# A recurrent attention layer on one core: the value pass in 32 rows, the memory-free tail tokens of four segments in one job, scores and softmax in two halves of the heads

## The chip, the cores and the metric

The kernel runs on one core of a Trainium2 chip. The metric is device time in microseconds for the whole program. "TensorE" is the matmul engine (PE in the profile, PEld its weight loads), VectorE is DVE, ScalarE is ACT, GpSimd is POOL, SP issues most of the DMAs.

## The reference, cut to what matters

Four layers, A B A B, on 2048 tokens of width 640. Layer A is not touched. Layer B is a recurrence over 64 segments of 32 tokens. Eight memory tokens stand before each segment, and the first eight output rows of a segment are the next segment's memory:

```
for s in range(64):
    h = concat([mem, x[32*s : 32*s+32]])          # 40 tokens, width 640
    q, k, v = h @ Wq, h @ Wk, h @ Wv              # 32 heads of 128 each
    p = softmax(mask(q k^T * scale))              # 40 x 40 per head
    o = (p v) @ Wo
    mem = o[:8];  outs.append(o[8:])
```

Only `mem` ties a step to the next. What depends on `x` alone can be computed ahead.

## The kernel before

Thirty-two stationary columns (tokens) use a quarter of TensorE's 128 columns, so four matmuls with different weights stand side by side (`tile_position`). Such a "thin group" of 20 matmuls covers half of one weight matrix:

```python
def thin_mm(cols_ap, Wt, b, name):                # 32 tokens, half b of the weights
    ps = ps_tile([128, 512], F32, name)
    for c in range(NCH):                          # 5 chunks of 128 of the width 640
        for j in range(4):
            n = 4 * b + j
            nc.tensor.matmul(ps[32*j:32*j+32, :], lhsT=cols_ap[:, c, :], rhs=Wt[:, c, 512*n:512*n+512],
                             start=(c == 0), stop=(c == NCH-1), tile_position=(0, 32*j), ...)
```

Queries and keys of a step are made for 32 columns: the 8 memory tokens, and the first 24 tokens of the *next* segment. The last 8 tokens of each segment (the "tail") come from a separate job, two segments at a time, half of it in each step as filler (`b_tps`). Values need all 40 tokens at once, so they go in 64 columns, two matmuls side by side, in four quarters:

```python
def v_quarter(b4):
    vps = ps_tile([128, 512], F32, "b_VPS")
    for c in range(NCH):
        for jj in range(2):
            n = 2 * b4 + jj
            nc.tensor.matmul(vps[64*jj:64*jj+64, :], lhsT=hT[s][:, c, 0:64], rhs=W.wv[:, c, 512*n:512*n+512],
                             start=(c == 0), stop=(c == NCH-1), tile_position=(0, 64*jj), ...)
```

The order of one step on TensorE, with the tile names that the profile shows:

```
Qa Qb Ka Kb | VPS 0 | TPQ | VPS 1 | TPK | SP (mask, scores) of both halves | VPS 2, 3
| tps | PTP (transposes of P) | tps | OTP (P times V) | OPS (output pass) | ttp | MT (memory to hT) | XPS (fold)
# every fourth step, serially after it:
| OPSd (output pass of the eight rows per segment that OPS leaves out, four segments at once) | wait for ScalarE | XPSd (fold)
# cut: softmax on VectorE, ScalarE and GpSimd, copies out of PSUM, DMAs
```

OPS handles 32 of a segment's 40 rows: the memory and 24 tokens. The other eight rows are collected over four segments; their OPSd is called the deferred pass below. MT writes the new memory into the next step's `hT`, and the next Qa waits for it. That is the recurrence.

Of the kernel before, what the change touches and what calls it, by code (L numbers as in the profile page):

```python
# [8 lines left out]
"""Dev version of the kernel (layer A / layer B building blocks)."""  # L9
# [19 lines left out]
D = 640  # L29
# [461 lines left out]
def b_group_of_head(h):  # L491
    pr = h // 2
    u, v = divmod(pr, 4)
    return 4 * u + (0, 2, 1, 3)[v]


def layer_B(nc, tc, C, W, x_src, xb_src, x_dst, mem0, nsteps=64, out_bf16=False, dbg=None):
    SCB = 1.0 / math.sqrt(128.0)
    nc_raw = nc
    nc = _OrdNC(tc, nc_raw, engines=ORDER_ENGINES)  # L500
    with ExitStack() as ctx:
        st = ctx.enter_context(tc.tile_pool(name="b_state", bufs=1))
        hp = ctx.enter_context(tc.tile_pool(name="b_hT", bufs=4))
        qkp = ctx.enter_context(tc.tile_pool(name="b_qk", bufs=4))
        wk = ctx.enter_context(tc.tile_pool(name="b_wk", bufs=1))
        wk2 = ctx.enter_context(tc.tile_pool(name="b_wk2", bufs=2))
        sm = ctx.enter_context(tc.tile_pool(name="b_sm", bufs=2))
# [8 lines left out]
        fold = st.tile([128, 2, 32], BF16, name="b_fold")  # L516
        nc.vector.tensor_tensor(out=fold[:, 0, :], in0=C.identb[:, 0:32], in1=C.identb[:, 64:96], op=ALU.add)
        nc.vector.tensor_tensor(out=fold[:, 1, :], in0=C.identb[:, 32:64], in1=C.identb[:, 96:128], op=ALU.add)
        OTdef = st.tile([128, 32, 32], BF16, name="b_OTdef")
        XO = st.tile([128, 320], F32, name="b_XO")  # L520
        nc.vector.memset(XO[:], 0.0)
        mask8 = st.tile([128, 8, 40], BF16, name="b_mask8")
        Pt = st.tile([128, 16, 64], BF16, name="b_P")
        nc.gpsimd.memset(Pt[:], 0.0)
# [4 lines left out]
        for hh in range(2):  # L529
            nc.gpsimd.affine_select(out=maskf[64 * hh:64 * hh + 32, 0:32], in_=negs[64 * hh:64 * hh + 32, :],  # L530
                                    pattern=[[1, 32]], compare_op=ALU.is_gt, fill=0.0, base=0, channel_multiplier=-1)
        nc.vector.tensor_copy(mask8[:], maskf[:].unsqueeze(1).to_broadcast([128, 8, 40]))

        xnT_g = {}
        ln_state = {}

        ln_dma = {}

        def ln_group_dma(g):
            xt = wk.tile([128, D], BF16, name="b_xt", tag="Qsb")  # L540
            nc.sync.dma_start(xt[:], xb_src[128 * g:128 * g + 128, :])
            ln_dma[g] = xt

        def ln_group_a(g):
            if g not in ln_dma:
                ln_group_dma(g)
            xt = ln_dma.pop(g)
            xn = wk.tile([128, D], BF16, name="b_xn", tag="PTsb")
            layernorm_tile(nc, sm, C, xt[:], xn[:], "b_ln")
            ln_state[g] = xn  # L550

        def ln_group_b(g):
            xn = ln_state.pop(g)
            tps = ps_tile([128, NCH, 128], BF16, "b_lntps")
            for c in range(NCH):
                nc.tensor.transpose(tps[:, c, :], xn[:, 128 * c:128 * c + 128], C.identb[:])
            xg = wk2.tile([128, NCH, 128], BF16, name="b_xnTg")
            nc.scalar.copy(xg[:], tps[:])
            xnT_g[g] = xg
# [5 lines left out]
        hT = {}  # L565
        QT = {}
        KT = {}

        def alloc_seg(s):
            hT[s] = hp.tile([128, NCH, 64], BF16, name="b_hT", tag="hT")  # L570
            QT[s] = qkp.tile([128, 32 * 40 + 24], BF16, name="b_QT", tag="QT")
            KT[s] = qkp.tile([128, 32 * 40 + 24], BF16, name="b_KT", tag="KT")
            nc.gpsimd.memset(QT[s][:, 1280:1304], 0.0)
            nc.gpsimd.memset(KT[s][:, 1280:1304], 0.0)
            nc.gpsimd.tensor_copy(hT[s][:, :, 0:32], xcols(s, 0, 32))
            if s >= 1 and (s - 1) in hT:
                nc.gpsimd.tensor_copy(hT[s - 1][:, :, 40:64], xcols(s, 0, 24))
            if s == nsteps - 1:
                nc.gpsimd.memset(hT[s][:, :, 40:64], 0.0)

        def thin_mm(cols_ap, Wt, b, name):
            ps = ps_tile([128, 512], F32, name)
            for c in range(NCH):
                for j in range(4):
                    n = 4 * b + j
                    nc.tensor.matmul(ps[32 * j:32 * j + 32, :], lhsT=cols_ap[:, c, :], rhs=Wt[:, c, 512 * n:512 * n + 512],
                                     start=(c == 0), stop=(c == NCH - 1), tile_position=(0, 32 * j), skip_group_check=True)
            return ps

        def evac(eng, dst, src, scale=None):  # L590
            if eng == "act":
                if scale is None:
                    nc.scalar.copy(dst, src)
                else:
                    nc.scalar.activation(out=dst, in_=src, func=ACT.Copy, scale=scale)
            elif eng == "dve":
                if scale is None:
                    nc.vector.tensor_copy(dst, src)
                else:
                    nc.vector.tensor_scalar(out=dst, in0=src, scalar1=scale, scalar2=None, op0=ALU.mult)  # L600
            else:
                nc.gpsimd.tensor_copy(dst, src)

        def transp4(sb_half, tp, b):
            for i in range(4):
                nc.tensor.transpose(tp[:, 4 * b + i, :], sb_half[:, 128 * i:128 * i + 128], C.identb[:])

        def scatter(eng, tp, b, dst_t, t0, t1, c0):
            src = tp[:, 4 * b:4 * b + 4, :].rearrange("p i (j t) -> p i j t", j=4)[:, :, :, t0:t1]
            dst = dst_t[:, 0:1280].rearrange("p (h c) -> p h c", c=40)[:, 16 * b:16 * b + 16, c0:c0 + (t1 - t0)] \  # L610
                .rearrange("p (j i) c -> p i j c", j=4)
            evac(eng, dst, src)

        def bulk_unit_pe(job, u):
            nm, b = (("Q", 0), ("Q", 1), ("K", 0), ("K", 1))[u]
            Wt = W.wq if nm == "Q" else W.wk
            job["ps"][u] = thin_mm(job["cols"], Wt, b, "b_tps")

        def bulk_unit_evac(job, u, eng):
            nm, b = (("Q", 0), ("Q", 1), ("K", 0), ("K", 1))[u]  # L620
            sb = wk.tile([128, 512], BF16, name="b_tsb", tag="tsb")
            evac(eng, sb[:], job["ps"][u][:], SCB if nm == "Q" else None)
            job["sb"][u] = sb

        def bulk_unit_tr(job, u):
            nm, b = (("Q", 0), ("Q", 1), ("K", 0), ("K", 1))[u]
            tp = ps_tile([128, 8, 128], BF16, "b_ttp")
            transp4(job["sb"][u][:], tp, 0)
            job["tp"][u] = tp

        def bulk_unit_scatter(job, u, eng):
            nm, b = (("Q", 0), ("Q", 1), ("K", 0), ("K", 1))[u]
            for (t0, t1, seg, c0) in job["dests"]:
                dst_t = (QT if nm == "Q" else KT)[seg]
                src = job["tp"][u][:, 0:4, :].rearrange("p i (j t) -> p i j t", j=4)[:, :, :, t0:t1]
                dst = dst_t[:, 0:1280].rearrange("p (h c) -> p h c", c=40)[:, 16 * b:16 * b + 16, c0:c0 + (t1 - t0)] \
                    .rearrange("p (j i) c -> p i j c", j=4)
                evac(eng, dst, src)

        def new_job(cols, dests):  # L640
            return {"cols": cols, "dests": dests, "ps": {}, "sb": {}, "tp": {}}

        def run_job_now(job):
            for u in range(4):
                bulk_unit_pe(job, u)
                bulk_unit_evac(job, u, "act" if u % 2 == 0 else "dve")
                bulk_unit_tr(job, u)
                bulk_unit_scatter(job, u, "dve" if u % 2 == 0 else "act")

        ln_group_a(0); ln_group_b(0)  # L650
        alloc_seg(0)
        with nc.allow_non_contiguous_dma(reason="mem0 transpose load (tiny)"):
            for c in range(NCH):
                nc.sync.dma_start(hT[0][:, c, 32:40], mem0[:, 128 * c:128 * c + 128].rearrange("t p -> p t"))
        if nsteps > 1:
            alloc_seg(1)
        run_job_now(new_job(hT[0][:, :, 0:32], [(0, 32, 0, 0)]))

        def make_tails_job(t):
            segs = [u for u in (t, t + 1) if u < nsteps]  # L660
            hx = wk.tile([128, NCH, 32], BF16, name="b_hx")
            nc.gpsimd.memset(hx[:], 0.0)
            dl = []
            for ii, u in enumerate(segs):
                nc.gpsimd.tensor_copy(hx[:, :, 8 * ii:8 * ii + 8], xcols(u, 24, 32))
                dl.append((8 * ii, 8 * ii + 8, u, 24))
            return new_job(hx[:], dl)

        if nsteps > 1:
            if nsteps > 2:  # L670
# [307 lines left out]
```

## Time and profile before

Median 3664.33 us (4 runs, 3661.93 to 3667.35).

| What | us | Where read |
|---|---|---|
| TensorE busy | 3322.3 of 3665.9 (91%) | page, part 1 |
| steps of layer B, in fours (the first listed is the second of a group) | 19.13, 19.13, 22.19, 19.26; mean 19.93 | timeline, start of Qa to start of Qa |
| 128 such steps | 2551, 70% of the span | product |
| value pass b_VPS | 626.3 | page, part 5 |

First the engines' busy time (page, part 1) and two costly groups (part 5: line, engine, operation, output from inputs, shapes, count, then busy us and mean ns of one, then idle time before them). All of layer B has line L103, a helper, so one goes by tile names.

```profile
PE 3322.3 (91%) x54915; PEld 2072.4 (57%) x54996; DVE 2032.6 (55%) x5299; ACT 1852.8 (51%) x4369; POOL 580.5 (16%) x1457
...
L103 PE MATMUL b_VPS<-b_wv,b_hT 128*64 128x512 bf16 x5120 | 626.3, 382 | 0.0
...
L103 PE MATMUL b_OPS<-b_wo,b_OTsb 128*32 128x320 bf16 x8192 | 304.5, 302 | 33.7 <-DVE b_OTsb L103 33.7
```

Now one step of the kernel before in the timeline, TensorE only, with some rows left out: start, duration, what, and in brackets how long the engine idled before it and for whom. It is one of the steps with the deferred pass.

```profile
1008.49 1.26 PE L103 MATMUL b_Qa<-b_wq,b_hT 128*32 128x512 bf16 x20
1009.57 1.25 PE L103 MATMUL b_Qb<-b_wq,b_hT 128*32 128x512 bf16 x20
...
1013.30 1.27 PE L103 MATMUL b_VPS<-b_wv,b_hT 128*64 128x512 bf16 x10
1014.50 0.62 PE L103 MATMUL b_TPQ<-c_identb,b_Qsb 128*128 128x128 bf16 x8
...
1018.12 2.35 PE L103 MATMUL b_VPS<-b_wv,b_hT 128*64 128x512 bf16 x20
1020.40 1.26 PE L103 MATMUL b_tps<-b_wq,b_hx 128*32 128x512 bf16 x20
1021.60 0.63 PE L103 MATMUL b_PTP<-c_identb,b_P 128*128 128x128 bf16 x8
1022.16 1.26 PE L103 MATMUL b_tps<-b_wq,b_hx 128*32 128x512 bf16 x20
1023.36 0.73 PE L103 MATMUL b_OTP<-b_PTsb,b_Vsb 40*128 40x40 bf16 x32
1024.31 2.36 PE L103 MATMUL b_OPS<-b_wo,b_OTsb 128*32 128x320 bf16 x64 [0.22 <-DVE b_OTsb L103]
...
1027.61 2.47 PE L103 MATMUL b_OPSd<-b_wo,b_OTdef 128*32 128x320 bf16 x64
1030.67 0.31 PE L103 MATMUL b_XPSd<-b_msbd,b_fold 128*32 128x320 bf16 x2 [0.59 <-ACT b_msbd L103]
1030.68 0.61 PE L103 MATMUL b_Qa<-b_wq,b_hT 128*32 128x512 bf16 x6
```

Read the *starts*, not the durations: matmuls are pipelined, and the last one's end is modelled. Qa starts at 1008.49 and Qb at 1009.57, so a thin group occupies TensorE for 1.08 us. A value quarter, half as many matmuls, takes as long: 64 columns allow two side by side, not four. When another tile shape follows, the same quarter needs 1.20 us (1013.30 to 1014.50). Between 1008.49 and 1030.68 hardly anything idles: TensorE carries the step. The deferred pass adds 3.06 us to every fourth step.

### The profile page before, as it was taken

What the parts mean: (1) busy time and instruction counts of PE and PEld (TensorE: products, weight loads), DVE (VectorE), ACT (ScalarE), POOL (GpSimd) and SP (SyncE); (2) the same over time, 40 slices, a digit from 0 to 9 for tenths busy, and PEclk for the clock granted to TensorE, in tenths of its full rate; (3) what the DMA queues carried; (4) which work ended last, traced back from release to release, by engine and by line L of the source; (5) the groups of instructions that cost most, each with busy time, mean ns of one, the idle gap of its engine ahead of it and who ended that gap; (6) DMA issues with size and microseconds to landing.
All of it is one profiled execution on the core that took longest, in us unless ns stands there. A gap on an engine that the chain in (4) does not pass through costs nothing.

```text
span 3665.9 us, 126295 instructions
## 1 busy us (share of the span) xinstructions
PE 3322.3 (91%) x54915; PEld 2072.4 (57%) x54996; DVE 2032.6 (55%) x5299; ACT 1852.8 (51%) x4369; POOL 580.5 (16%) x1457
## 2 busy tenths in 40 slices
PE   6988959999999999999869889599999999999998
PEld 4756635555555555555546666355555555555555
DVE  8888834444444444444479888344444444444444
ACT  5978824444444444444359788334444444444443
POOL 4233210110111111010122332101101110110100
PEclk9999979999999999999989999799999999999999
DMA  2010060000000000000020111600000000000000
GB/s 63 12 38 30 29 251 28 12 12 13 13 13 13 13 13 12 14 12 10 20 66 12 46 38 30 250 28 10 10 11 11 10 10 12 11 10 12 10 9 8
DMA packets 85997, 112.26 MB, mean 31 GB/s; under 512 B 27328, under 2 KB 75456, under 8 KB 81600
## 3 DMA queue, kind: packets, MB, share of 16 engines
q1 hardware_dynamic: 85440, 104.18, 9.0%
q8 instruction: 430, 7.05, 0.8%
q14 instruction: 127, 1.04, 0.1%
HBM read 72.13 MB, written 23.59 MB: 26 GB/s over the span
## 4 chain that ended last, share of the span: by engine, by line
PE 73%; ACT 12%; DVE 8%; issue 3%; DMA 2%; POOL 2%; SPq 0%; DVEq 0%; ACTq 0%; POOLq 0%
PE b_VPS L103 16%; PE b_tps L103 9%; PE b_OPS L103 8%; ACT a_Pj L338 5%; PE b_Qa L103 4%; PE b_Qb L103 4%; PE b_Ka L103 4%; PE b_Kb L103 4%; PE a_S L333 2%; ACT b_KT L103 2%; PE b_ttp L103 2%; PE b_PTP L103 2%; PE b_TPK L103 2%; PE b_TPQ L103 2%; PE b_OPSd L103 2%
## 5 line engine op out<-in xcount | busy, mean ns | idle before, releaser
L103 PEld LDWEIGHTS <-b_hT 128*32 128x32 bf16 (+1 forms) x15520 | 609.3, 102 | 499.2 <-issue 102.1
L103 PE MATMUL b_VPS<-b_wv,b_hT 128*64 128x512 bf16 x5120 | 626.3, 382 | 0.0
L338 ACT ACTIVATE a_Pj<-a_S,a_negm 128x128 bf16<-128x128 f32 (+3 forms) x1024 | 504.1, 541 | 49.1 <-DVE a_negm L337 42.9
L337 DVE TENSOR_REDUCE a_negm<-a_S 128x1 f32<-128x128 f32 (+3 forms) x1024 | 466.9, 481 | 76.8 <-PE a_S L335 48.8
L103 ACT CAST b_Vsb<-b_VPS 128x512 bf16<-128x512 f32 x512 | 289.3, 594 | 179.6 <-PE b_VPS L103 179.6
L103 POOL TENSOR_TENSOR b_P<-b_P,b_rs 128x320 bf16<-128x320 bf16 x128 | 92.4, 722 | 1799.7 <-DVE b_rs L103 1785.1
L103 PE MATMUL b_OPS<-b_wo,b_OTsb 128*32 128x320 bf16 x8192 | 304.5, 302 | 33.7 <-DVE b_OTsb L103 33.7
L103 PEld LDWEIGHTS <-b_OTsb 128*32 128x32 bf16 x8192 | 208.4, 97 | 99.9 <-DVE b_OTsb L103 46.8
L348 PE MATMUL a_tpA<-c_identb,a_Pj 128*128 128x128 bf16 x2048 | 232.1, 220 | 7.9 <-ACT a_Pj L338 2.8
L335 PE MATMUL a_S<-c_negu,c_identb 128*128 128x128 bf16 x1024 | 221.3, 219 | 0.0
L103 PEld LDWEIGHTS <-b_hx 128*32 128x32 bf16 x5120 | 114.0, 97 | 151.1 <-issue 56.0
L103 DVE CAST b_Ksb<-b_Kb 128x512 bf16<-128x512 f32 x128 | 88.5, 692 | 187.7 <-PE b_Kb L103 187.7
L103 DVE CAST b_OTsb<-b_OTP 128x320 bf16<-128x320 f32 x256 | 114.1, 486 | 141.4 <-PE b_OTP L103 141.0
L103 DVE COPY b_QT<-b_TPQ 128x128 bf16<-128x128 bf16 (+1 forms) x254 | 62.1, 286 | 231.3 <-ACT b_QT L103 231.3
L103 DVE TENSOR_SCALAR b_Qsb<-b_Qb 128x512 bf16<-128x512 f32 x128 | 88.5, 692 | 163.9 <-PE b_Qb L103 163.9
L103 ACT CAST b_Ksb<-b_Ka 128x512 bf16<-128x512 f32 x128 | 74.9, 585 | 206.7 <-PE b_Ka L103 206.7
L348 PEld LDWEIGHTS <-a_Pj 128*128 128x128 bf16 x2048 | 146.7, 97 | 50.3 <-issue 10.1
L103 PE MATMUL b_Qa<-b_wq,b_hT 128*32 128x512 bf16 x2560 | 167.3, 384 | 3.1
L335 PEld LDWEIGHTS <-c_identb 128*128 128x128 bf16 x1024 | 99.4, 97 | 124.7 <-issue 94.9
L103 PE MATMUL b_Qb<-b_wq,b_hT 128*32 128x512 bf16 x2560 | 165.7, 382 | 0.0
L103 PE MATMUL b_tps<-b_wq,b_hx 128*32 128x512 bf16 x2560 | 164.9, 387 | 0.0
L103 PE MATMUL b_Ka<-b_wk,b_hT 128*32 128x512 bf16 x2560 | 164.0, 379 | 0.0
(1623 smaller groups left out, 6161.5 us busy)
## 6 DMA issues: line engine op xcount, KB each, us to landing
xres<-a_xnew SPq DMA_DIRECT2D x32, 320.0 KB
b_wq<-in_B_Wq_dram SPq DMA_DIRECT2D x2, 5120.0 KB
b_wk<-in_B_Wk_dram SPq DMA_DIRECT2D x2, 5120.0 KB
b_wv<-in_B_Wv_dram SPq DMA_DIRECT2D x2, 5120.0 KB
b_wo<-in_B_Wo_dram SPq DMA_DIRECT2D x2, 5120.0 KB
b_XO<-xres SPq DMA_DIRECT2D x256, 30.0 KB
xres_bf<-a_xnb SPq DMA_DIRECT2D x32, 160.0 KB
b_xt<-xres_bf SPq DMA_DIRECT2D x32, 160.0 KB
```

The lines of the kernel that those rows point to most:

```text
L103: r = f(*a, **k)
L333: nc.tensor.matmul(Sx[:, 0:N], lhsT=stt["qTm"][:, j, 128 * qc:128 * qc + 128], rhs=kT[:, 0:N], start=True, stop=False)
L335: nc.tensor.matmul(Sx[:, N - 128:N], lhsT=C.identb[:], rhs=C.negu[:], start=False, stop=True)
L337: nc.vector.tensor_reduce(out=negm[:], in_=Sx[:, 0:N], axis=AX.X, op=ALU.max, negate=True)
L338: nc.scalar.activation(out=Pj[:, OFFS[qc]:OFFS[qc] + N], in_=Sx[:, 0:N], func=ACT.Exp, bias=negm[:, 0:1], scale=1.0)
L348: nc.tensor.transpose(tpA[:, bi, :], Pj[:, OFFS[qc] + 128 * kc: OFFS[qc] + 128 * kc + 128], C.identb[:])
```

## The change

Its intent is less TensorE time per step. (1) The tails of *four* segments (4 x 8 = 32 tokens) become one job, now for V too, so that the values of a step need only 32 columns: 24 tokens and the memory. (2) The deferred output pass becomes filler of the next step. The filler is then about equal in all four steps: deferred pass, V tails, Q tails, K tails. (3) Scores and softmax run in two halves of the heads, so that the first half's softmax lies behind other work. P times V then has two parts per head, 32 and 8 rows. The fold matmuls give way to a second addition on VectorE. The diff, cut to its core:

```diff
-            def v_quarter(b4): ...                       # 64 columns, four quarters
+            vcols = lambda c: hT[s][:, c, 0:32]
+            Va, vparts = thin_parts(vcols, W.wv, 0, "b_V")      # 32 columns, two halves
...
-        def make_tails_job(t):                               # two segments, Q and K
+        class TailUnit:                                      # four segments, Q, K or V, one half; run part by part
...
-            if s % 4 == 3 or last:
-                opsd = o_pass(lambda h: OTdef[:, h, :], "b_OPSd")     # serial
+            if i4 == 0:
+                units = [deferred.pop(T - 1)] if T >= 1 else []        # filler of the next step
+            elif T + 1 < NT:
+                kind = " VQK"[i4]
+                units = [TailUnit(T + 1, kind, 0, "act"), TailUnit(T + 1, kind, 1, "dve")]
...
+            Qa; Ka; Qb; TPQa; TPKa; Kb                       # condensed: calls and evacuations left out
+            scores(0)
+            TPQb; Va; soft_1(0); TPKb; Vb parts 0 to 2
+            scores(1)
+            soft_2(0); soft_1(1); Vb parts 3, 4
+            fill(5); soft_2(1)
+            ptp = ptrans(0); fill(2)
+            ptp = ptrans(1); fill(3)                         # 10 filler parts in all, 0.216 us each
...
-                            nc.tensor.matmul(otp[:, k, q, :], lhsT=Vsb[64 * jj:64 * jj + 40, b4, ...],
+                                nc.tensor.matmul(otp[jj][:, b, r, :], lhsT=V_[32 * j:32 * j + n_, b, ...],   # n_ = 32, then 8
+                                                 rhs=PTsb[32 * j:32 * j + n_, ...], start=(k == 0), stop=(k == 1), tile_position=(32 * j, 0))
...
+            nc.vector.tensor_tensor(out=XO[0:64, :], in0=ops[0:64, :], in1=XO[0:64, :], op=ALU.add)
+            nc.vector.tensor_tensor(out=XO[0:64, :], in0=ops[64:128, :], in1=XO[0:64, :], op=ALU.add)
```

## The prediction

> **What bounds the kernel now.** The page gives TensorE 3322 of 3666 us busy (91%); the chain of waits is 73% PE. Layer B runs twice, 64 recurrent steps each. In the timeline a step (Qa start to Qa start) repeats in fours: 19.13, 19.13, 22.19, 19.26 us, mean 19.93; the 22.19 holds the serial deferred output pass. 128 x 19.93 = 2551 us, about 70% of the span. Inside a step TensorE issues nearly without gaps; the longest are about 0.3 us (for OTsb, for hT) and 0.6 us once in four (XPSd). VectorE and ScalarE are below half busy. Layer A is untouched.
>
> **Removed and added on TensorE, per step, issue times from the timeline.** Twenty 32-column matmuls (a "thin group") take 1.08 us; ten 64-column matmuls of a value quarter take 1.08 us too.
> - Value pass: four quarters, 4.32 us, become two thin groups, 2.16: -2.16.
> - Tail jobs: two thin groups per step (Q and K) become six per four steps (Q, K, V), 1.62: -0.54. Half of the ttp transposes go: -0.22.
> - Fold matmuls XPS go: -0.2. The deferred pass no longer stands alone: its 2.16 us of work stays as filler, but its wait for msbd and the second fold (about 0.9 us per four steps) go: -0.2.
> - PV: 32 matmuls of 40 rows (0.6 us) become 64 of 32 and 8 rows in alternating row groups: +0.3 (0 to +0.7).
> - More tile-shape changes. The Trainium skill, "TensorEngine Tiling (Array Packing)", Key Properties, says that changing the tiling mode drains TensorE. The trace agrees in size: a thin group followed by another shape takes 1.18 to 1.20 us instead of 1.08. Splitting into halves adds about five: +0.6.
>
> Net about -2.4 us of TensorE time per step.
>
> **What is given back.** With less filler, the softmax of the second half shows. The operations from the trace in the new order (reduce 0.48, add 0.50, exp 0.44, sum 0.48, reciprocal 0.20, two multiplies about 0.6, with 0.03 to 0.15 us between engines): scores(1) end near 9.1 us into the step, P of the second half is ready near 12.1, but TensorE reaches its transposes (PT1) near 11.6. Estimated stall 0.5 to 0.8 us. The waits for OTsb (0.1 to 0.3), msb (0.2) and hT (0.35) stay. My hand schedule from these durations gives 18.4 to 18.7 us per step, against 19.93. All of it is on the critical path, because PE carries the step: -1.45 us x 128 = -185 us. The prologue gains two serial groups per layer: about +4 us.
>
> **Prediction:** 3482 us (5.0% faster), 8 in 10 between 3420 and 3540. Chance of faster by over 2%: 0.95; within 2%: 0.04; slower: 0.01.
>
> **What would show it right.** Steps nearly equal (18.2 to 18.8 us), the 22 us step gone. TensorE busy falls by about 300 us, more than the span; its share drops to about 87%. The V groups (b_V) take about half of b_VPS's 626 us. In the waits, PE or its weight loads wait for VectorE's b_P, 0.4 to 0.9 us per step, where before they waited for POOL's b_P. PV lasts 0.7 to 1.3 us.
>
> **What would make it wrong.** (1) PV row groups running one after another at over 20 ns each, or with drains between 32- and 8-row matmuls: over +1 us. (2) VectorE order: the KT scatter for the next step and PTsb sit between P and the PV; if they delay PTsb, PV starts late. (3) Mode changes dearer than 0.12 us. (4) The eight-token V transfers (four per step) landing late: a DMA wait at PV. (5) A PSUM bank held by the deferred pass stalling later matmuls. On the other side, if the second half's softmax hides fully, 17.7 us per step, 3380 us.

## The result, and the profile after

3443.48 us median (4 runs, 3441.07 to 3447.04) against 3664.33. The ratio is 0.9393, 95% interval 0.9378 to 0.9408. Ratios here are the mean time of one kernel's fast runs over that of the other's of the same rounds, so not quite the ratio of the medians. The gain of 6.1% was forecast as 5.0%, and 3443 lies inside the stated range. The page after, the same parts:

```profile
PE 3017.7 (88%) x56899; PEld 1780.5 (52%) x56980; DVE 2075.8 (60%) x5369; ACT 1691.9 (49%) x3987; POOL 660.2 (19%) x1687
...
L103 PE MATMUL b_OPS<-b_wo,b_OTsb 128*32 128x320 bf16 x8192 | 318.5, 310 | 44.3 <-DVE b_OTsb L103 44.3
L103 PE MATMUL b_V<-b_wv,b_hT 128*32 128x512 bf16 x5120 | 346.9, 382 | 0.0
```

TensorE lost 304.6 us of busy time and the span 220.6 us; the value pass alone gave 279 us of the busy time (626.3 to 346.9; the V tails are counted elsewhere). The steps are now 17.84, 17.90, 17.88, 18.15 us (first to fourth of a group), mean 17.94; in the same order they were 19.26, 19.13, 19.13, 22.19. One step after the change in the timeline, TensorE, the third of four (Q tails as filler):

```profile
1026.81 1.26 PE L103 MATMUL b_Qa<-b_wq,b_hT 128*32 128x512 bf16 x20 [0.28 <-DVE b_hT L103]
...
1032.84 1.26 PE L103 MATMUL b_V<-b_wv,b_hT 128*32 128x512 bf16 x20
1034.04 0.40 PE L103 MATMUL b_TPK<-c_identb,b_Ksb 128*128 128x128 bf16 x4
1034.37 0.83 PE L103 MATMUL b_V<-b_wv,b_hT 128*32 128x512 bf16 x12
1035.13 0.31 PE L103 MATMUL b_SP<-b_mask,c_identb 128*128 128x320 bf16 x1
1035.37 0.43 PE L103 MATMUL b_SP<-b_KT,b_QT 128*64 128x40 bf16 x16
1035.73 0.62 PE L103 MATMUL b_V<-b_wv,b_hT 128*32 128x512 bf16 x8
1036.17 1.25 PE L103 MATMUL b_tail<-b_wq,b_hx 128*32 128x512 bf16 x20
1037.36 0.40 PE L103 MATMUL b_PTP<-c_identb,b_P 128*128 128x128 bf16 x4
1037.69 0.61 PE L103 MATMUL b_tail<-b_wq,b_hx 128*32 128x512 bf16 x8
1038.67 0.42 PE L103 MATMUL b_PTP<-c_identb,b_P 128*128 128x128 bf16 x4 [0.37 <-DVE b_P L103]
1039.03 0.83 PE L103 MATMUL b_tail<-b_wq,b_hx 128*32 128x512 bf16 x12
1041.05 2.36 PE L103 MATMUL b_OPS<-b_wo,b_OTsb 128*32 128x320 bf16 x64 [0.37 <-DVE b_OTsb L103]
```

A value half now costs 1.08 us plus a change of shape (1032.84 to 1034.04). TensorE waits 0.37 us for P of the second half, the wait that the forecast named. The waits of TensorE, by whom it waited for (total us, times, longest), in the first layer B after the change (window 640 to 1700 us, about 59 steps):

```profile
PE b_OPS L103 <- DVE b_OTsb L103: 20.7, 59, 0.4
PE b_PTP L103 <- DVE b_P L103: 20.5, 45, 2.0
PE b_MT L103 <- ACT b_msb L103: 16.5, 31, 0.5
PE b_Qa L103 <- DVE b_hT L103: 16.3, 59, 0.3
```

Each is a wait of 0.3 to 0.5 us that comes up in nearly every step, for P in three of four, for msb in half of them. But the longest wait for P is 2.0 us, and so another line needs a look: where the time went that the steps saved and the span did not.

| Piece (timeline) | before | after | difference |
|---|---|---|---|
| start to first Qa of layer B | 549.64 | 556.60 | +7.0 |
| 63 steps, first B | 1255.6 | 1138.0 | -117.7 |
| last step, layer A, start of second B | 580.4 | 584.8 | +4.4 |
| 63 steps, second B | 1254.1 | 1138.9 | -115.2 |
| last Qa to the end | 26.2 | 27.1 | +0.9 |

A saving of 1.99 us would make 125 us over 63 steps (123 us, as the step left out is a long one), not 116. The missing part is at the edges: step 0 gained nothing (21.67 and 21.64 us; in the second B it lost, 20.45 and 22.33), and the steps 61 and 62, which have no filler because no further segments follow, take 19.46 and 19.96 us (first B). They have 2.16 us *less* work than their neighbours and take up to 2 us *longer*. The timeline of step 61 of the second B, TensorE:

```profile
3387.73 0.41 PE L103 MATMUL b_PTP<-c_identb,b_P 128*128 128x128 bf16 x4
3390.12 0.61 PE L103 MATMUL b_PTP<-c_identb,b_P 128*128 128x128 bf16 x4 [1.99 <-DVE b_P L103]
```

And the view of windows there: length, busy time of each engine with its instruction count, then the granted TensorE clock (the 0.99 and 0.50), DMA share and GB/s.

```profile
3387.70:3390.10 2.40, 0.43 (x8) 0.23 (x4) 1.73 (x6) 1.30 (x3) 0.09 (x1) 0.99 0.05 9
3390.10:3391.10 1.00, 0.86 (x19) 0.69 (x21) 0.96 (x4) 0.01 (x1) 0.00 (x0) 0.50 0.00 0
3392.50:3394.50 2.00, 1.95 (x32) 1.20 (x36) 0.39 (x1) 0.35 (x1) 1.48 (x7) 0.50 0.07 16
3397.50:3399.00 1.50, 1.19 (x22) 0.72 (x26) 0.92 (x3) 0.17 (x1) 0.00 (x0) 1.00 0.00 0
```

After an idle stretch of 2 us, the clock is half for about 7 us in this step, and the output pass in it takes 4.46 us instead of 2.36. So filler may do two things: hide the softmax, and keep the clock up. That was not in the forecast, and it is one of the questions for the experiments.

### The profile page after: what moved, and what is told of

Read it like the earlier page. It is cut to its first block, busy times and chain, and to the rows that moved or that the text cites. A ratio compares the mean times of both kernels' runs of the same rounds, so it can differ in the third digit from the quotient of the medians.

```text
span 3445.3 us, 130756 instructions
## 1 busy us (share of the span) xinstructions
PE 3017.7 (88%) x56899; PEld 1780.5 (52%) x56980; DVE 2075.8 (60%) x5369; ACT 1691.9 (49%) x3987; POOL 660.2 (19%) x1687
## 5 line engine op out<-in xcount | busy, mean ns | idle before, releaser
L103 PEld LDWEIGHTS <-b_hT 128*32 128x32 bf16 x15520 | 356.2, 96 | 376.9 <-DVE b_hT L103 46.6
L103 PE MATMUL b_V<-b_wv,b_hT 128*32 128x512 bf16 x5120 | 346.9, 382 | 0.0
L103 POOL TENSOR_TENSOR b_P<-b_Pu,b_rs 128x256 bf16<-128x256 bf16 (+1 forms) x256 | 111.2, 455 | 1181.9 <-DVE b_rs L103 1181.9
L103 ACT ACTIVATE b_Pu<-b_SP 128x320 bf16<-128x320 f32 x256 | 111.9, 437 | 357.3 <-DVE b_SP L103 357.3
L103 ACT COPY b_QT<-b_TPQ 128x128 bf16<-128x128 bf16 x508 | 178.3, 379 | 119.7 <-PE b_TPQ L103 115.9
L103 DVE COPY b_KT<-b_TPK 128x128 bf16<-128x128 bf16 x382 | 101.7, 266 | 218.6 <-PE b_TPK L103 218.6
L103 DVE CAST b_Ksb<-b_Ka 128x512 bf16<-128x512 f32 x128 | 88.5, 691 | 149.9 <-PE b_Ka L103 149.6
L103 ACT ACTIVATE b_Qsb<-b_Qb 128x512 bf16<-128x512 f32 x128 | 76.4, 597 | 198.1 <-PE b_Qb L103 198.1
L103 DVE TENSOR_REDUCE b_negmax<-b_SP 128x8 f32<-128x320 f32 x256 | 124.8, 487 | 71.1 <-PE b_SP L103 71.1
L103 DVE TENSOR_REDUCE b_ssum<-b_Pu 128x8 f32<-128x320 bf16 x256 | 123.1, 481 | 72.4 <-ACT b_Pu L103 72.4
```

The costliest lines, as they stand in the source:

```text
L103: r = f(*a, **k)
```

## The experiments

The theory (A): TensorE carries the step almost everywhere; the gain is the TensorE time removed, less the changes of tile shape added and less a wait for the second half's P. The rivals: the gain came from the order and the filler rather than the value pass; the changes of shape cost nothing, as the waits swallow them; the deferred pass was the main thing. Each kernel was timed in three rounds against the kernel before, and all gave the right result. "After" below is 3443 us; its repeat in the last batch (e10) gave 3445.05. Kernels of different batches ran with kernels before of 3664 to 3668 us (medians), so differences of under about 6 us between batches are not read.

### e2: the value pass issued twice

```diff
-            for f in vparts:
+            for f in vparts + vparts:          # first half; the second half likewise
                 f()
```

> The changed kernel with every value group issued twice (the second run overwrites the first, the result stays right): 2.16 us more TensorE work per step, as much as the old 64-row value pass had. Theory A (value pass is on the path of TensorE): +2.0 to +2.2 us per step, 3700 to 3725 us, slower than the kernel before. Rival (the value pass lies in the shadow of the softmax, the gain came from the tail jobs, the deferred pass and the order): under +1 us per step, below 3570 us.

Measured: 3718.29 us, ratio to before 1.0142 (1.0123 to 1.0161). Steps 20.00, 20.03, 20.03, 20.31: +2.13 to +2.16 us, of 2.16 added. The value pass lies wholly on TensorE's path. With the old amount of value work, the changed kernel is *slower* than the kernel before. So the value pass in 32 rows is worth more than the whole net gain; the rest of the change, in this order, costs some 52 us more than it saves (3718 against the 3666 of its own batch). That is the gross worth: the V tails, which the narrow value pass needs (two thin groups per four steps, 0.54 us per step, an estimate of 69 us over 128 steps), and the second part of PV are counted with the rest.

### e4: one more thin group as filler

```diff
+            extra = thin_parts(tail_cols(T), W.wv, 0, "b_extra")[1]     # five parts, result unused
             def fill(k):
+                # 2, 1 and 2 of them before the filler parts of fill(5), fill(2), fill(3)
```

> The changed kernel with one more thin group (five parts, 1.08 us, result unused) per step, spread 2, 1, 2 over the three filler places. If TensorE carries the step even between scores(1) and PV: +0.75 to +1.08 us per step, +95 to +138 us, 3540 to 3580 us. If the softmax of the second half carries it there: under +0.4 us per step, below 3495 us.

Measured: 3508.18 us, +65, between the two. Steps 18.44, 18.55, 18.49, 18.77: +0.6 us for 1.08 us of work. The wait for P fell from 50.1 us in all to 9.9 us. Both expectations missed: the time lies between them. So in the stretch between scores(1) and PV neither bound holds alone: about 0.45 us of work per step fits in free (the wait of 0.37 us with its shape change), and what goes beyond it is paid in full. e2's work, placed earlier, got nothing free.

### e3: two changes of tile shape fewer

```diff
+            mask_in(0)       # mask matmul beside the transposes TPKa, same 128-column shape
             ...
-                nc.tensor.matmul(sp[:], lhsT=C.identb[:], rhs=mask ...)   # was first in scores(b)
+            mask_in(1)       # beside TPKb
```

> The changed kernel with each mask matmul moved next to the transposes of the same tile shape, so that two changes of tile shape per step fall away; same work. If a change of shape costs 0.10 to 0.12 us of TensorE time on the path: -0.20 to -0.24 us per step, -26 to -31 us, about 3415 us. Rival (the cost is swallowed by the waits for P, OTsb and msb that follow): within 8 us of 3443.

Measured: 3426.55 us, -17. Steps 17.63, 17.80, 17.66, 18.05 against 17.84, 17.90, 17.88, 18.15: -0.21, -0.10, -0.22, -0.10. The first and third steps show the full price of two changes, 0.1 us each. In the fourth, only one change falls away, because the layer-norm transposes stand just before and share the mask's shape. In the second, TensorE now waits longer for `b_hx`, a copy on GpSimd that was issued late (total 9.3 to 12.7 us). So the rival falls; the forecast's size was right per change, its count was not.

### e1 and e6: the deferred pass serial again, without and with useless filler

```diff
 # e1
-                units = [deferred.pop(T - 1)] if T >= 1 else []
+                units = []                     # first step of four has no filler
...
-            if last:
+            if i4 == 3:                        # pass runs alone at the end of every fourth step
                 od = deferred.pop(T); od.run(100); store_deferred(T, od)
 # e6 = e1 and
+                idle = thin_parts(..., "b_idle")[1] + thin_parts(..., "b_idle")[1]    # 10 parts, result unused, at the three filler places
```

> The changed kernel, but the deferred output pass stands alone again at the end of every fourth step, and the step after it has no filler. Theory A (filler both covers the softmax wait of the second half and keeps TensorE at full clock): the two steps per pass of the changed kernel that have no filler take 19.5 and 20.0 us with b_OPS at 4.5 instead of 2.4 us, so every first step of four goes from 17.85 to about 19.9 us and every fourth from 18.15 to about 20.4; 32 groups x 4.2 us = +135 us, about 3578 us. Theory B (filler only covers the wait, the clock does not matter): the first step stays at 17.9, the fourth takes 20.4: +70 us, about 3515 us. Theory C (the work is only moved): within 20 us of 3443.

> The run e1 (3548 us, first step of four 19.3 us) with ten parts of unused thin matmuls (2.16 us of useless work) as filler in the emptied step. If TensorE slows its clock after the 2 us wait for P: the first step goes back to 17.9 us, b_OPS there to 2.4 us: -1.4 to -1.5 us x 32, about 3502 us, faster by doing more. If the clock does not matter: not faster than 3548 us.

Measured: e1 3548.04 us, e6 3496.46 us. e6 does 2.16 us *more* on TensorE in every fourth step and is 52 us faster. Steps: e1 about 19.3, 17.93, 17.87, 19.99; e6 17.80, 17.93, 17.87, 19.99. The emptied step of e1 in the timeline, TensorE:

```profile
1023.93 0.42 PE L103 MATMUL b_PTP<-c_identb,b_P 128*128 128x128 bf16 x4 [1.96 <-DVE b_P L103]
1026.23 3.91 PE L103 MATMUL b_OPS<-b_wo,b_OTsb 128*32 128x320 bf16 x64 [0.29 <-DVE b_OTsb L103]
```

And its window while the clock was half (columns as above; the granted clock is the 0.50):

```profile
1026.10:1029.40 3.30, 3.17 (x48) 1.86 (x52) 0.47 (x2) 0.39 (x2) 1.65 (x7) 0.50 0.12 23
```

The same step of e6:

```profile
1009.15 0.42 PE L103 MATMUL b_PTP<-c_identb,b_P 128*128 128x128 bf16 x4 [0.37 <-DVE b_P L103]
1009.51 0.83 PE L103 MATMUL b_idle<-b_wv,b_hx 128*32 128x512 bf16 x12
1011.47 2.36 PE L103 MATMUL b_OPS<-b_wo,b_OTsb 128*32 128x320 bf16 x64 [0.31 <-DVE b_OTsb L103]
```

Theories B and C of e1 fall. Theory A was right in kind but too large (+105 us, not +135): the half clock lasted 3.4 us in 28 of the 30 emptied steps after step 0 and about 6.8 us only in the other two, so the first step came to 19.3 and not 19.9 us, and the fourth to 19.99 and not 20.4. Without filler, TensorE waits 1.96 us for P, and then the output pass runs at 3.91 us; with useless matmuls in the wait it runs at 2.36 us, and the trace shows no half clock in that step. So moving the deferred pass into the filler was worth 105 us in the changed kernel, of which about 52 us (e1 less e6: the second transposes of P start about 11.85 us into the step in both) is the clock. The Trainium skill, "TensorE: Matmul & The Clock Gate", Part 1, describes such a gate; its numbers agree with these in part (see the end).

### e5: the kernel before with the deferred pass as filler, alone

```diff
+            if s % 4 == 0 and s > 0:                        # in the next step, before the PV matmuls
+                opsd_prev = o_pass(lambda h: OTdef[:, h, :], "b_OPSd")
...
-            if s % 4 == 3 or last:                          # serial
```

> The kernel before with one part of the change alone: the deferred output pass is no longer serial after every fourth step but runs before the PV matmuls of the next step. Theory A (TensorE carries the step; only the wait for msbd and the fold, about 0.9 us per pass, goes, plus what little wait it covers): 0.9 to 1.2 us per four steps, -29 to -38 us, about 3630 us, within 2% of before. Rival (the 22.19 us step was a serial tail that filler hides wholly): -3 us per four steps, -96 us, about 3568 us.

Measured: 3645.44 us, ratio 0.9940 (0.9921 to 0.9958). The saving of 22 us is less than the 29 to 38 expected, and far from the rival's 96. The fourth step falls from 22.19 to 19.45, but the next rises from 19.26 to 21.31. In the kernel before TensorE does not wait at that place, so filler has nothing to fill; only the wait for msbd and some overlap are saved. Much the same edit (here the second fold stays) is worth 22 us there and 105 us after the change. What an edit is worth depends on what else the step holds.

### e7, e8, e9: a version that beats both

The waits that remain in the profile after suggest the next edits. e7 is e3 and an order in which scores(1) come before most of the value pass, so that the softmax of the second half starts about 1.2 us earlier, behind most of the value work; VectorE takes the second half's maximum before the first half's sum; the copy `b_hx` is issued early. e8 moves filler parts into the waits for OTsb, msb and hT. e9 reorders the start of the layer and gives the steps without filler useless matmuls.

```diff
 # e7
-            scores(0); TPQb; Va; soft_1(0); TPKb; Vb[:3]; scores(1); soft_2(0); soft_1(1); Vb[3:]
+            scores(0); TPQb; max(0); TPKb; exp(0); Va[:2]; scores(1); max(1); exp(1); soft_2(0); Va[2:]; Vb
+            if i4 == 1: tail_cols(T + 1)                    # b_hx early
 # e8 = e7 and
-            fill(5) ... ptrans(0); fill(2); ptrans(1); fill(3); PV; OPS; msb; MT; hT
+            fill(4..6) ... ptrans(0); ptrans(1); fill(3); PV; fill(1); OPS; msb; fill(1) or ln_tr or ttp; MT; hT; fill(rest)
 # e9 = e8 and
-        for kind in ("Q", "K", "V"): tails ...; then first-segment Q, K; then layer norm of group 1
+        Q tails, layer norm of group 1, Q of segment 0; K tails, K of segment 0; V tails      # in the order in which weights land
+            idle = [] if units else ...                     # unused matmuls in steps without filler
```

> e3 (3427 us) plus the order: the transposes of K's second half and scores(1) come before most of the value pass, VectorE does the maximum and subtraction of the second half before the sum of the first, and the copy for the V tail columns is issued early. If the softmax of the second half still costs TensorE time at PT1 (0.44 us per step) and the rest of the order is free: about 17.2 to 17.4 us per step against 17.8, -55 to -75 us, about 3360 us. Rival (nothing to gain, TensorE already carries the step alone): within 15 us of 3427.

> e7 plus filler moved to the waits that no order removed: one part between PV and the output pass (wait for OTsb, 0.3 us), one part or the layer-norm transposes before MT (wait for msb, 0.5 us in the first two of four steps), one before Qa (wait for hT, 0.28 us), the P transposes side by side. My schedule from trace durations gives 16.6 to 16.8 us per step: about -80 us against e7, 3270 to 3300 us. If filler there delays the chain as much as it saves: within 20 us of e7.

> e8 (3276 us) plus two repairs that the traces suggest. Start of a layer: the jobs that need only the weights of Q and K run while the next weights are still on their way (TensorE waited 17.6, 5.8 and 5.2 us there), so step 0 starts about 12 us earlier, twice. First step and last three steps of a layer, which have no filler: unused matmuls as filler keep the clock up; steps of 19.6, 18.2, 17.9 and the last one should go to about 17, some 5 us per layer. Together -25 to -35 us, about 3246 us. If the start is bound by the last weights alone and the clock is not the cause: within 8 us of 3276.

> The changed kernel unaltered, on the same chip and in the same rounds as e9, to give the ratio of the two: 3443 us within 0.3%.

| Run | median us | ratio to before (95%) | steps in fours, us |
|---|---|---|---|
| after | 3443.48 | 0.9393 (0.9378 to 0.9408) | 17.84, 17.90, 17.88, 18.15 |
| e7 | 3352.75 | 0.9143 (0.9127 to 0.9159) | 17.27, 17.32, 17.32, 17.49 |
| e8 | 3275.62 | 0.8928 (0.8915 to 0.8941) | 16.64, 16.61, 16.76, 16.76 |
| e9 | 3248.67 | 0.8864 (0.8850 to 0.8877) | the same; step 0 16.69 instead of 19.59 |
| e10 (after again) | 3445.05 | 0.9400 (0.9385 to 0.9416) | |

The totals of all three came out as expected. In e8 the output pass starts without a wait and the P transposes stand together (timeline, TensorE, rows left out):

```profile
1016.29 1.91 PE L103 MATMUL b_V<-b_wv,b_hT 128*32 128x512 bf16 x32
1018.03 1.47 PE L103 MATMUL b_tail<-b_wk,b_hx 128*32 128x512 bf16 x24
1019.43 0.62 PE L103 MATMUL b_PTP<-c_identb,b_P 128*128 128x128 bf16 x8
1019.98 0.83 PE L103 MATMUL b_tail<-b_wk,b_hx 128*32 128x512 bf16 x12
1021.57 0.40 PE L103 MATMUL b_tail<-b_wk,b_hx 128*32 128x512 bf16 x4
1021.95 2.36 PE L103 MATMUL b_OPS<-b_wo,b_OTsb 128*32 128x320 bf16 x64
```

The wait for P has gone from this step: the value pass and the filler cover the softmax. e7 also shows that a wait of 2 us is not needed for the half clock. In its step 62, which has no filler, the longest wait before the output pass is 0.69 us (the first line is from the timeline, the others are windows, with the granted clock third from the end):

```profile
1640.86 0.29 PE L103 MATMUL b_PTP<-c_identb,b_P 128*128 128x128 bf16 x2 [0.69 <-POOL b_P L103]
1639.30:1642.70 3.40, 2.05 (x43) 1.05 (x35) 2.86 (x10) 2.16 (x5) 1.11 (x2) 1.00 0.00 0
1642.80:1646.10 3.30, 3.11 (x82) 2.06 (x85) 0.89 (x2) 0.79 (x2) 1.08 (x3) 0.50 0.03 5
```

TensorE was busy for 2.05 of 3.40 us there, in short waits, and then had half the clock for 3.4 us.

e9's first Qa starts at 547.96 us instead of 555.20, 7 us and not the 12 that I expected; in the second B, from the last Qa of the first B to its own first Qa takes 567.47 us instead of 580.52, 13 us less. Step 0 (2.9 us) and the last steps (about 16.6 instead of 18.2 and 17.9) add some 5 us per layer. In the profiled runs that makes 30 us, in the medians 27. e9 bundles the two repairs, so their shares are read from the timeline, not from separate runs.

## Why the prediction was right

- **TensorE carries the step: shown.** e2 turned 2.16 us of added work into 2.15 us of step.
- **Value pass -2.16 us: right.** e2 adds the same amount back and pays it in full; b_VPS to b_V fell by 279 us, 2.2 us per step.
- **Deferred pass: the forecast (its work stays, its waits go) holds for the kernel before** (e5: 22 us). It missed that in the new order filler at this place is also what keeps the clock at full (e1 and e6).
- **PV +0.3 us: a little less.** The 64 matmuls start within 0.72 us (1039.79 to 1040.51 in the trace), the 32 of before within 0.56 us: +0.16. Within one row group the starts are 25 ns apart, also between 32 and 8 rows, so there is no drain; those of the other row group start 1 to 5 ns after them.
- **Changes of shape, 0.12 us each: shown at about 0.1** (e3: 0.21 and 0.22 us for two). The Trainium skill, "TensorEngine Tiling (Array Packing)", Key Properties, says that a change of mode drains the array; this trace agrees in kind, and the page has no number, so the forecast's "agrees in size" has nothing on the page behind it.
- **Wait for P, 0.5 to 0.8 us per step: mis-sized.** It was 0.37 us in three steps of four and nothing in the second, where TensorE waits for `b_hx` first. This term, PV and the changes of shape made the forecast of 18.4 to 18.7 us per step too long; 17.94 was measured. That is also outside the 18.2 to 18.8 named as a sign of being right. The forecast's own terms do not add up to its time either: -2.4 us and +0.5 to 0.8 for the wait give -1.6 to -1.9 us, while the hand schedule that it used gives -1.45; where the rest lies is not in the text.
- **The waits that "stay": wrong in kind, small in size.** Before, TensorE's idle time over the steps 4 to 59 of the first B was 0.74 us per step, without any wait for msb or hT; after, it is 1.26 us (OTsb 0.36, P 0.29, hT 0.28, msb 0.27, `b_hx` 0.08). So 2.5 us of work went and 0.5 us of waits came; the forecast had 2.4 and, by its steps, about 0.95. The work was forecast well, what is given back was taken too large.
- **The named dangers did not occur.** TensorE shows no wait of note for the V tail transfers, for a PSUM bank or for PTsb (0.8 us in all in that window of the first B).
- **Edges: +4 us was forecast, +12.3 us came** (7.0, 4.4 and 0.9 in the table). Layer A, which is the same code, varies by about 2 us from run to run: in the repeat e10 the same sum is 6.8 us. From the last matmul of A to the first Qa of B, without A, it is 54.2 and 55.9 us before, 61.5 and 62.6 after, 61.1 and 61.6 in e10: 6 to 7 us more per layer. The steps 61 and 62 took back 3.6 and 4.2 us per layer more. So two errors partly cancelled: the steps gained more than forecast (1.99 instead of 1.45 us), the edges gave back more. The sum, 220 instead of 181 us, stayed in the range; that it came so near is in that part luck.

Step 0's slowness after the change is the clock, twice. TensorE waits 2.79 us for the layer norm just before it, then Qa and Ka take 1.8 and 2.1 us from start to start instead of 1.1 (granted clock 0.50 for 3.4 us); later, after 1.99 us of waiting for P, the clock is half for 6.8 us. e6, whose step 0 has useless filler, loses only the first of the two: 19.50 instead of 21.64 us.

What stays open: the 32-row value pass and the two halves of the softmax were never put into the kernel before alone. e2 prices the value pass inside the new order; what the halves and the order are worth by themselves is not shown.

## What to carry to other kernels

When one in-order engine carries a recurrence, count its time from start to start in the timeline and price every removed group so; then walk the new order once with the durations of the other engines to find which wait comes up. Give each wait some work of the same tile shape, in the size of the wait: spread well, the same work here cost 16.7 us per step instead of 17.9. Look at the granted clock wherever the matmul engine waits a good part of the time: here it fell to half after one wait of 2 us, and also after several short ones that left it busy for 2.05 of 3.40 us (e7). If there is no useful filler, useless matmuls can pay for themselves (e6: more work, 52 us less), and it is worth looking for steps that are slower *because* they have less to do.

## What the Trainium skill lacked or had wrong

- "TensorE: Matmul & The Clock Gate", Part 1 and "Why this matters for your kernels": these two places set the limit at an idle window of about 3.4 us and advise against idle gaps over about 3 us. Here less was enough: one gap of 1.96 to 1.99 us between two short groups of transposes (0.99 before it, 0.50 after), and in e7 short waits with a longest of 0.69 us, 2.05 of 3.40 us busy. Transposes are counted as busy in these figures; no run shows whether the gate counts them so. Only these two places are meant: other sections of the page bear on short idles and on transposes. The way back, about 3.4 us of sustained work in Part 1, agrees with 28 of 30 emptied steps of e1 (3.4 us at half); in the other two, and in the step 61 shown above, it took about 7 us although TensorE was busy for most of it.
- The same page, "Wait — 56ns, not 53.3ns?", gives a floor of about 25 ns from start to start for small matmuls. The trace agrees within one row group (25 ns). That section does not say that the floor is one of each row group (the page's part on packing treats tiles side by side): with two row groups side by side, 64 matmuls of 40 columns started within 0.72 us, about 11 ns each.
- "TensorEngine Tiling (Array Packing)", Key Properties: that a change of mode drains the array is stated without a price. Here it was about 0.1 us per change (1.20 instead of 1.08 us for a group followed by another shape; e3: 0.21 to 0.22 us per step for two changes).
- No page tells that a step can get faster when useless matmuls are put into a wait, as e6 did (52 us).
